# Unread products of the identity in TensorE's pauses, and a new order of all work, in an attention and two-MLP kernel

## The chip, the cores and the metric

The kernel runs on one core of a Trainium2 chip. The metric is the device time of one execution in microseconds. Three runs of the kernel before took 716.44, 717.51 and 718.22 us; the median is 717.51 us.

## The reference, cut to what matters

Three stages follow one another. The first is an attention in both directions between 512 tokens and 32 states, for 4 batches and 8 heads of 64; the other two are MLPs on the 2176 rows that come out of it (4 x 512 tokens and 4 x 32 states, 512 wide).

```python
scores = scale * x @ state.T          # tokens read states, softmax, times state
scores2 = scale * state @ x.T         # states read tokens, softmax, times x
x = concatenate([xread, sread], axis=2)      # 4 x 544 rows of 512
h = x @ w_in                                 # 512 x 2048
x = softplus(h) @ w_out                      # 2048 x 512
g = x @ w_gate; v = x @ w_val                # 512 x 1536 each
out = (silu(g) * v) @ w_out2                 # 1536 x 512
```

The weights are float64 in memory.

## The kernel before, in words

**Arithmetic.** A float32 matrix product is made of three products in a faster format (float32r): each operand is split into a high part (ScalarE copies it into that format) and a low part (VectorE or GpSimd subtracts), and high x high, low x high and high x low are summed. Such a product of 128 x 128 by 128 x 512 is three matmul instructions; a "group" here is six of them (two such products). The weights come as float64, as two 32-bit words each; the steps `size`, `bits` (ScalarE), `head` and `tail` (VectorE) put a float32 together from them before it is split. In the short names of the order these are `ab`, `bt`, `hd`, `tl`, then `wh` (high) and `wl` (low). Some blocks of the MLPs use a scheme with seven products in place of eight, with sums of operands (`g`, `yt`, `at`, `ws`, `sm`).

**The attention.** Items are pairs of a batch (0 to 3) and a parity of heads, numbered 0 to 7: item k is batch k // 2. The steps of an item are, by their short names in the order and their lines: `sc` (L599, TensorE: scores; float32 matmuls, two instructions each, of the two halves of x that `x00` to `x31` load), `mx` and `nm` (L605, L608, VectorE: maximum and its negative), `e` (L612, ScalarE: exponential and its sum), `rc` (L618, L619, VectorE: reciprocals of both items of a batch), `ts` (L625, VectorE: the scores transposed in squares of 32), `M` (L628), `mi` (L632, GpSimd or VectorE: minus the maximum), `ex` (L637, ScalarE), `S` (L640), `r` (L644, L645), `ti` (L649, GpSimd or VectorE), `tu` (L655, transposed back), `ah` (L659, ScalarE: high part), `al` (L662, GpSimd or VectorE: low part); and for the states `pa` (L667, TensorE: four transposes with the identity), `a` (L671, ScalarE), `pr` (L679, TensorE: 16 small products with x in its other layout, `n00` to `n31`), `sr` (L688, ScalarE), `st` (L692, TensorE) and `so` (L698, ScalarE).

**The first MLP.** The attention's last product is folded into the first weights: `mm.cb` (L708, TensorE) multiplies the states of batch b with the c-th 512 columns of w_in, `mh` and `ml` (L712 on ScalarE, L716 on VectorE) split the result. Unit n stands for 512 of these columns c, a batch b and 128 columns of them; `p` n (L756) makes its product (six matmuls, operands from `mh`, `ml`, `ah`, `al`), `sp` n (L738, L743, ScalarE) the softplus, `gl` n (L764, GpSimd) its low part, and `P` n (L780, or L890 in the seven-product scheme) the product with w_out; `ya` to `yd` add the results to the accumulators (L792, L794). `p0` to `p3`, the units of the first batch, are the first split products of the kernel; `P0` follows them. The states take a path of their own (`s1`, L948; `s3`, L968).

**The second MLP.** The `q` products (L1005) take the weights of gate and value from a copy that the kernel has written to DRAM in split form and reads back (`lg`, L518, four loads of 512 KB; `lw`, L522, and `ls`, L568, for the last weights). `a`, `b`, `c` steps and `as`, `bs`, `cb` (L1247, L1264, L1266, L1270) form silu(g) * v, `th` and `tL` (L1011, L1018) split it, `om` (L1042) and `op` (L1066) multiply it with w_out2 and `oA`, `oa` (L1030) add. The path of the states is L1090 to L1130.

**The order.** ORDER is a written-out list of all steps, made ahead of time, and it is the order of every engine's queue and of the DMA queue of SyncE (SP), which starts all loads and stores (L382 and L386 for x, L396 for the weights, `ld.` in the order). Each engine works through its own steps in that order and waits where an operand is not there. A `!` behind a name sends a step to the other of its two engines: steps that are on GpSimd by default (`mi`, `ti`, `al`, `wl`, `sm`, `sl`, `gl`, `gL`, `yl`, `tL`, `wsl`, `cb`, `os.l`, `os.s`) go to VectorE, those on VectorE by default (`ws`, `g`, `yt`, `at`, `os.w`) to GpSimd. HOMES says where each tile lies: eight PSUM banks (`b`), and rooms in SBUF of two sizes (`k`, `d`). Tiles on one line of HOMES share a room one after the other, so a load waits in SP's queue until the tile before it in its room has been read.

Of the kernel before, what the change touches and what calls it, by code (L numbers as in the profile page):

```python
# [17 lines left out]
P = 128  # L18

ORDER = (  # L20
# [174 lines left out]
    ),  # L195
# [1172 lines left out]
```

## Time and profile before

| | |
|---|---|
| median of three runs | 717.51 us (716.44 to 718.22) |
| the profiled execution | 716.6 us, its span 714.8 us |
| TensorE matmuls busy | 699.1 us (98%) |
| VectorE, ScalarE, GpSimd busy | 577.3, 400.3 and 144.6 us |
| moved by DMA | 134.88 MB |

The span is the time from the first to the last instruction on the core; the execution's own time has 1.8 us more around it. PE is TensorE's matmuls, PEld its loading of the stationary operand, DVE is VectorE, ACT ScalarE, POOL GpSimd, SP SyncE's queue. "idle before" is the time that an engine stood before an instruction, with what released it. The granted clock is given as a share of 2.4 GHz, so that 0.50 is 1.2 GHz.

### The profile page before, as it was taken

How to read it: one execution, taken by the hardware profiler on the slowest of the kernel's cores; microseconds unless marked ns; L12 is line 12 of the kernel's file. 1: busy time of each engine (PE TensorE's matmuls, PEld its weight loads, DVE VectorE, ACT ScalarE, POOL GpSimd, SP SyncE). 2: the span in 40 equal slices, each digit the busy share in tenths (PEclk: the TensorE clock that was granted, in tenths of full speed). 3: DMA queues.
4: the chain of work that ended last, by engine and by line, in shares of the span. 5: the costliest groups of instructions: out<-in, count | busy, mean ns of one | idle time of the engine just before them, and what ended most of it. 6: DMA issues, size and time to landing. Idle time of an engine off the chain costs nothing.

```text
span 714.8 us, 10171 instructions
## 1 busy us (share of the span) xinstructions
PE 699.1 (98%) x3618; PEld 555.9 (78%) x3618; DVE 577.3 (81%) x993; ACT 400.3 (56%) x740; POOL 144.6 (20%) x122
## 2 busy tenths in 40 slices
PE   5999999999999999999999999999999999999997
PEld 1478877786878777888888888888888788888886
DVE  4886735899999999889768788868986789967776
ACT  3897664767676767567555654654543344333231
POOL 0244324223562314150101000001020210101101
PEclk9699999999999999999999999999999999999999
DMA  8970000334342500454864757565959889974603
GB/s 336 380 282 19 1 1 28 92 111 156 117 147 91 200 36 1 142 211 149 292 237 157 255 207 277 217 224 209 318 181 351 309 316 357 323 263 160 277 1 118
DMA packets 48626, 134.88 MB, mean 189 GB/s; under 512 B 5440, under 2 KB 17728, under 8 KB 48576
## 3 DMA queue, kind: packets, MB, share of 16 engines
q1 hardware_dynamic: 48576, 134.24, 52.8%
q8 instruction: 28, 0.46, 0.3%
q14 instruction: 22, 0.18, 0.1%
HBM read 93.06 MB, written 41.16 MB: 188 GB/s over the span
## 4 chain that ended last, share of the span: by engine, by line
PE 92%; DVE 3%; DMA 3%; ACT 1%; issue 0%; SPq 0%; ACTq 0%; DVEq 0%
PE b L1005 31%; PE b L890 16%; PE b L756 12%; PE b L1042 11%; PE b L1066 6%; PE b L780 6%; PE b L1090 2%; PE b L948 2%; PE b L708 2%; PE b L968 2%; PE b L1123 1%; DMA k<-gv_d 1%; DMA k<-in_xn_dram 1%; DMA k<-in_xt_dram 1%; PE b L599 1%
## 5 line engine op out<-in xcount | busy, mean ns | idle before, releaser
L1005 PE MATMUL b<-k,k 128*128 128x512 f32 x1008 | 242.6, 391 | 0.6 <-DMA k<-gv_d 0.5
L1005 PEld LDWEIGHTS b<-k,k 128*128 128x128 f32 x1008 | 187.8, 188 | 40.7 <-DMA k<-gv_d 1.0
L890 PE MATMUL b<-d,k 128*128 128x512 f32 x454 | 113.1, 392 | 0.3 <-DVE k L794 0.3
L890 PEld LDWEIGHTS b<-d,k 128*128 128x128 f32 x454 | 84.4, 188 | 24.1 <-issue 3.4
L756 PE MATMUL b<-k,k 128*128 128x512 f32 x384 | 94.8, 393 | 0.0
L1247 DVE TENSOR_TENSOR d<-b,d 128x512 f32<-128x512 f32 x96 | 65.3, 685 | 27.2 <-PE b L1005 16.8
L1264 ACT ACTIVATE d<-b 128x512 f32<-128x512 f32 x72 | 42.4, 593 | 79.2 <-PE b L1005 65.1
L756 PEld LDWEIGHTS b<-k,k 128*128 128x128 f32 x384 | 71.2, 188 | 18.8 <-issue 3.4
L1030 DVE TENSOR_TENSOR k<-b,k 128x512 f32<-128x512 f32 x110 | 73.5, 684 | 14.6 <-PE b L1042 8.4
L1042 PE MATMUL b<-d,k 128*128 128x512 f32 x336 | 82.2, 390 | 0.0
L1042 PEld LDWEIGHTS b<-d,k 128*128 128x128 f32 x336 | 62.8, 188 | 13.0
L1011 ACT ACTIVATE d<-d 128x512 fp32r<-128x512 f32 x63 | 38.4, 625 | 45.7 <-DVE d L1247 34.4
L764 POOL TENSOR_TENSOR d<-d,d 128x512 fp32r<-128x512 f32 x31 | 43.6, 1418 | 93.0 <-ACT d L743 36.8
L419 DVE SCALAR_TENSOR_TENSOR d<-d,k 128x512 int32<-128x512 int32 x66 | 47.3, 727 | 18.3 <-ACT k L413 18.2
L794 DVE TENSOR_TENSOR k<-b,k 128x512 f32<-128x512 f32 x84 | 56.2, 683 | 5.0 <-PE b L890 4.6
L432 ACT ACTIVATE k<-d 128x512 fp32r<-128x512 f32 x51 | 32.0, 629 | 36.9 <-DVE d L426 13.8
L1066 PE MATMUL b<-d,k 128*128 128x512 f32 x210 | 52.0, 390 | 0.0
L1066 PEld LDWEIGHTS b<-d,k 128*128 128x128 f32 x210 | 39.3, 188 | 8.5 <-DVE k L1030 0.4
L1018 DVE TENSOR_TENSOR d<-d,d 128x512 fp32r<-128x512 f32 x55 | 40.5, 739 | 6.6 <-ACT d L1011 6.4
L780 PE MATMUL b<-d,k 128*128 128x512 f32 x192 | 45.1, 390 | 0.0
L413 ACT ACTIVATE k<-k 128x512 int32<-128x512 uint32 x68 | 44.9, 673 | 0.0
L780 PEld LDWEIGHTS b<-d,k 128*128 128x128 f32 x192 | 35.8, 188 | 7.6 <-POOL d L764 0.2
(175 smaller groups left out, 949.1 us busy)
## 6 DMA issues: line engine op xcount, KB each, us to landing
k<-gv_d SPq DMA_DIRECT2D x60, 512.0 KB, 7.9
gv_d<-k SPq DMA_DIRECT2D x48, 512.0 KB, 3.5
k<-in_moe_w_out_dram SPq DMA_DIRECT2D x28, 512.0 KB, 5.3
k<-w_d SPq DMA_DIRECT2D x23, 512.0 KB, 7.6
k<-in_moe_w_in_dram SPq DMA_DIRECT2D x16, 512.0 KB, 6.5
k<-in_moe_w_gate_dram SPq DMA_DIRECT2D x48, 128.0 KB, 3.5
k<-in_moe_w_val_dram SPq DMA_DIRECT2D x48, 128.0 KB, 3.6
w_d<-k SPq DMA_DIRECT2D x12, 512.0 KB, 3.8
```

Of the source, the lines that this page charges most:

```text
L413: nc.scalar.activation(self.bot, low_word, AF.Copy, bias=-0.5 + 7.5 * 2.0 ** -18, scale=2.0 ** -29 * (1 - 2.0 ** -18),)
L419: nc.vector.scalar_tensor_tensor(out=ti, in0=ti, scalar=3, in1=self.bot, op0=ALU.logical_shift_left, op1=ALU.bitwise_or,)
L756: nc.tensor.matmul(ps, halves[s3], others[t3], start=par == 0 and n3 == 0, stop=par == NPAR - 1 and n3 == 2)
L764: eng.tensor_tensor(out=l, in0=sp[u].g, in1=sp[u].h.bitcast(F32), op=ALU.subtract)
L780: nc.tensor.matmul(yps[c, b, dt], halves[s3], t[t3], start=ft == 0 and n3 == 0, stop=ft == FT - 1 and n3 == 2)
L794: nc.vector.tensor_tensor(out=v, in0=ps, in1=v, op=ALU.add)
L890: nc.tensor.matmul(ps, halves[s3], g[t3], start=part in OPENS and f == 0 and n3 == 0, stop=f == 1 and n3 == 2, skip_group_check=True)
L1005: nc.tensor.matmul(ps, halves[s3], others[t3], start=first and i == 0 and n3 == 0, stop=i == 1 and n3 == 2, skip_group_check=True)
L1030: nc.vector.tensor_tensor(out=v, in0=ps, in1=v, op=ALU.add)
L1042: nc.tensor.matmul(ps, halves[s3], act[n + f, j][t3], start=f == 0 and n3 == 0, stop=f == 1 and n3 == 2)
L1066: nc.tensor.matmul(ps, halves[s3], act[n, t][t3], start=opens and n3 == 0, stop=n3 == 2, skip_group_check=True)
L1247: eng.tensor_tensor(out=o(), in0=x(), in1=y(), op=op)
```

## The change

**Unread products.** A step `warm.N.NAME` multiplies the 128 x 128 identity with itself N times (float32) into the bank of the tile NAME, which nothing reads before the tile's own first product overwrites it. There are six in the order: `warm.5.sc0_0` ahead of `sc0`, `warm.8.pa2_1` ahead of `pa5`, `warm.2.pa1_0` ahead of `pa2`, `warm.5.pr2_0` ahead of `pr4`, `warm.1.pm0_0_0` ahead of `mm.00` and `warm.2.pr1_0` ahead of `pr2`; 23 products.

**The order and the homes.** The list has the same 2235 steps beside these six, in another order, and every tile may have another home (41 large rooms and 20 small ones, where there were 40 and 21). 96 steps change between VectorE and GpSimd: 55 go to GpSimd and 41 to VectorE.

**The first addition to an accumulator** is found from the order (the first step that comes) and no longer from the column block c.

The diff, cut to the new function and the part of the order up to the first split products:

```diff
 ORDER = (
-    "x00 st x01 x20 x21 x10 ld.w00 x11 ld.w03 x30 sc0 x31 sc1 ts0 mx0 ld.w02 sc5 nm0 M0 e0 mi0! ld.w01 mx1 ex0 sc4",
-    "mx5 n20 nm1 nm5 S0 e5 pa0 mx4 e1 pa5 nm4 ts5 a0 n21 ab.w00 pa1 ts4 e4 ts1 n11 a5 pa4 rc4 M1 a1 sc3 M5 bt.w00",
-    "mi1 n00 M4 a4 sc2 ab.w03 mx3 mi4 n01 sc6 bt.w03 ts3 ex4 nm3 mx2 ex1 ts2 n10 e3 nm2 S1 e2 pa3 mx6 sc7 n31",
-    "ab.w02 r0 bt.w02 pa2 nm6 mx7 e6 hd.w03 ld.o00 ab.w01 pa6 nm7 ti1! e7 hd.w02 bt.w01 pa7 hd.w00 pr4 a2 hd.w01",
-    "ld.o01 a3 n30 pr5 tu1 sr4 a7 mm.00 rc2 M2 a6 ld.o03 mi2! sr5 mh.000 st2 pr3 M3 so2 mh.001 mm.02 rc0 mi3 ld.o02",
-    "ml.000 ex2 mh.020 S2 ti0 pr0 mh.021 ts7 pr1 ah1 mi5 ts6 mm.01 ex3 ml.001 sr1 al1 sr0 tu0 ex5 pr2 ml.021 sr3",
-    "ah0 st0 pr7 sr2 al0! so0 mh.011 st1 p0 ld.o12 rc6 S3 so1 ld.w11 ab.o00 ml.011 ld.o10 bt.o00 p2 ld.o11 sr7",
-    "hd.o00 ab.o01 ld.w12 r2 wh.o00 p1 S5 ti2 sp0 ml.020 pr6 ti3! p3 wl.o00! ld.w20 ld.e1.0 tu2 sr6 gl0 bt.o01 tu3",
...
+    "x00 st x01 x20 x21 ld.w00 ld.w03 x10 x11 x30 warm.5.sc0_0 sc0 x31 sc1 ts0 mx0 ld.w02 sc4 nm0 mx1 e0 ld.w01 nm1",
+    "M0 pa0 e1 sc5 mx4 a0 n20 rc0 ab.w00 mx5 bt.w00 nm5 nm4 ts4 n21 e5 ts5 e4 warm.8.pa2_1 pa5 M4 n11 pa1 ab.w03",
+    "pa4 ts1 mi4 bt.w03 sc2 M1 a4 sc3 mi0 a5 mx2 a1 n10 mx3 sc6 mi1 ex0 n01 ts2 ex4 nm3 hd.w03 n00 e3 sc7 nm2 mx6",
+    "e2 rc4 n31 ex1 nm6 ts3 warm.2.pa1_0 pa2 pa3 ab.w02 M2 ld.o00 ab.w01 mx7 mi2 e6 S1 bt.w01 ld.o01 warm.5.pr2_0",
+    "pr4 nm7 hd.w00 pa6 bt.w02 S0 e7 pr5 hd.w02 sr4 pa7 r0 n30 a2 hd.w01 ld.w21 a7 ti1! a3 warm.1.pm0_0_0 mm.00 sr5",
+    "tu1 ld.o11 mh.000 M3 a6 pr3 rc6 mh.001 mi3 st2 ld.o12 mm.02 ml.000 so2 ah1 ts7 ti0 ex3 ld.o02 ts6 pr1 mh.021",
+    "al1 M5 pr0 mh.020 ld.o03 tu0 sr1 ex2 warm.2.pr1_0 pr2 rc2 ml.001 ah0 mm.01 ld.o10 sr3 al0! sr0 sr2 ml.021",
+    "ab.o00 st1 st0 pr7 mi5! bt.o00 p2 S2 ab.o01 S3 mh.011 p0 so0 hd.o00 so1 ex5 ml.011 ld.o13 wh.o00 ld.w11 r2 p1",
+    "sp0 ld.w12 ti2! ld.w20 wl.o00! pr6 ld.w10 ti3! p3 ml.020 sr6 gl0 bt.o01 sp1 P0 hd.o01 tu2 wh.o01 ld.w13 gl1",
...
     def y_add(c, b, dt):
-        y_put(b, dt, yps[c, b, dt], c == 0)
-
-    def y_put(b, dt, ps, first):
+        y_put(b, dt, yps[c, b, dt])
+
+    begun = set()
+
+    def y_put(b, dt, ps):
+        first = (b, dt) not in begun
+        begun.add((b, dt))
...
+        def warm(n, name):
+
+            ps = bank(name)
+            for _ in range(n):
+                nc.tensor.matmul(ps[:, :P], ident, ident, start=True, stop=True)
+
+        for names in ORDER:
+            for name in names.split():
+                if name.startswith("warm."):
+                    op(name, warm, int(name.split(".")[1]), name.split(".")[2])
```

The loads `lg13`, `lg15`, `lg16`, `lg21`, `lg1`, `lw0`, `lw12`, `lw13` and `ls0`, of which the prediction speaks, stand in the second half of the order.

## Rows read from the trace of the kernel before

**Rows 1.** The page, part 1: busy time of each engine.

```profile
PE 699.1 (98%) x3618; PEld 555.9 (78%) x3618; DVE 577.3 (81%) x993; ACT 400.3 (56%) x740; POOL 144.6 (20%) x122
```

**Rows 2.** Busy time by stage: stretch, length, engines, granted clock, DMA share, GB/s.

```profile
9.84:39.10 29.26, 24.59 (x355) 11.41 (x352) 25.91 (x57) 23.36 (x53) 6.44 (x6) 0.77 0.89 348
...
140.00:340.00 200.00, 199.42 (x996) 157.00 (x995) 188.69 (x308) 136.57 (x248) 66.41 (x55) 1.00 0.36 123
```

**Rows 3.** TensorE's three waits from 39 us on, first and last: total, times, longest.

```profile
PE b L1005 <- DMA k<-gv_d: 0.5, 1, 0.5
...
PE b L890 <- ACT d L864: 0.3, 1, 0.3
```

**Rows 4.** TensorE by stretch of the attention: length, busy, granted clock, DMA share, GB/s.

```profile
4.83:13.40 8.57, 7.44 (x36) 1.00 0.99 374
...
16.90:30.20 13.30, 11.60 (x89) 0.50 0.99 389
31.00:39.10 8.10, 7.28 (x211) 1.00 0.63 235
```

**Rows 5.** Forms on TensorE in 0 to 13.4, 13.6 to 16.8, 16.9 to 30.2 us: busy, mean ns.

```profile
L599 PE MATMUL b<-k,d 64*32 64x512 f32 x32 | 6.4, 1056 | 6.0 <-DMA d<-in_st_dram 4.8 <-DMA k<-in_xt_dram 1.1
...
L667 PE MATMUL b<-ident,d 128*128 128x128 f32 x8 | 1.3, 287 | 1.5 <-ACT d L612 1.5
...
L599 PE MATMUL b<-k,d 64*32 64x512 f32 x32 | 5.6, 1058 | 0.0
```

**Rows 6.** Timeline of VectorE in the attention: start, length, instruction, idle before.

```profile
9.84 0.72 DVE L625 STREAM_TRANSPOSE d<-b 128x512 f32<-128x512 f32 x1 [9.84 <-PE b L599]
...
12.56 1.28 DVE L605 TENSOR_REDUCE mx<-b 128x1 f32<-128x512 f32 x2
...
20.54 0.69 DVE L605 TENSOR_REDUCE mx<-b 128x1 f32<-128x512 f32 x1 [0.93 <-PE b L599]
...
25.89 0.69 DVE L605 TENSOR_REDUCE mx<-b 128x1 f32<-128x512 f32 x1 [1.06 <-PE b L599]
...
37.78 0.69 DVE L662 TENSOR_TENSOR k<-d,k 128x512 fp32r<-128x512 f32 x1 [0.32 <-ACT k L659]
38.39 0.16 DVE L618 TENSOR_SCALAR sm<-sm 128x2 f32<-128x2 f32 x1
```

**Rows 7.** Timeline of TensorE in the attention and at the first split product.

```profile
18.54 3.67 PE L599 MATMUL b<-k,d 64*32 64x512 f32 x24
...
25.73 1.97 PE L667 MATMUL b<-ident,d 128*128 128x128 f32 x8
...
32.78 1.09 PE L708 MATMUL b<-d,d 64*32 64x512 f32 x16
33.80 1.10 PE L679 MATMUL b<-k,d 128*32 128x64 f32 x64
...
39.10 4.38 PE L756 MATMUL b<-k,k 128*128 128x512 f32 x18
```

**Rows 8.** Timelines of ScalarE and of GpSimd: `ah0`, and `gl0` ahead of P0.

```profile
37.13 0.62 ACT L659 ACTIVATE k<-d 128x512 fp32r<-128x512 f32 x1
...
44.63 1.30 POOL L764 TENSOR_TENSOR d<-d,d 128x512 fp32r<-128x512 f32 x1 [1.54 <-ACT d L743]
```

**Rows 9.** The chain that ended last, 76 to 84 us: 32 float32 matmuls of 128 columns.

```profile
79.74 3.57 PE b L948 x32
```

**Rows 10.** The same chain, 555 to 580 us, and the page's loads: KB, us to landing.

```profile
554.80 6.35 PE b L1005 x28
...
563.88 6.61 DMA k<-gv_d
...
k<-gv_d SPq DMA_DIRECT2D x60, 512.0 KB, 7.9
```

**Rows 11.** Timeline of VectorE: one L419 alone, one while GpSimd works.

```profile
40.79 0.69 DVE L419 SCALAR_TENSOR_TENSOR d<-d,k 128x512 int32<-128x512 int32 x1 [0.86 <-ACT k L413]
...
45.44 1.04 DVE L419 SCALAR_TENSOR_TENSOR d<-d,k 128x512 int32<-128x512 int32 x1
```

More of the change, by code (lines that the diff above doesn't have):

```diff
@@ L893, in y_part_add @@
         j, m = TO[part]
-        y_put(2 * q + j, 2 * m + i, ypx[c, q, part, i], c == 0 and part in ("P1", "P5", "P6", "P4"))
+        y_put(2 * q + j, 2 * m + i, ypx[c, q, part, i])
     ysum = {}
```

520 rows, old and new, of tables (HOMES, ORDER) are left out of this document.

## The prediction

> **What bounds the kernel now.** I read the page's totals first, then the stages, then TensorE's own waits, and last the attention, instruction by instruction. TensorE is busy for 699.1 us of the 714.8 us span [rows 1], so only what shortens its work or its pauses can shorten the run. After the first split product (L756, at 39.10 us [rows 7]) its pauses that carry a releaser come to 1.1 us in three waits [rows 3]. Everything else, some 14 us of pauses and of slow running, lies ahead of 39.10 us. What follows is a fixed list of products, the same in both kernels: whatever makes the first product start earlier moves the whole list, one for one, as long as the list then runs without new pauses.
>
> So the question is what holds the first product back. In the stage up to it VectorE is busy 25.91 us of 29.26, ScalarE 23.36, and TensorE is "busy" 24.59 at a mean granted clock of 0.77 [rows 2]. The clock column says 1.00 up to 13.4 us, 0.50 from 16.9 to 30.2, 1.00 from 31 [rows 4]. The durations correct the first of these: a score matmul takes 1056 ns before 13.4 us and 1058 ns where 0.50 is granted, while the transposes between 13.6 and 16.8 us take 287 ns and four of them up to 1 us in the slow stretch [rows 5, 7]. TensorE therefore worked at 1.2 GHz in both, and at 2.4 GHz only from about 13.6 to 16.9 us and again from 31. The Trainium skill's TensorE: Matmul & The Clock Gate (Part 1, Seeing it yourself) warns not to trust every clock event of a trace; by that, too, the durations decide. The same page calls the cost of the slow start under 1% of a typical span, which as an estimate would be a ceiling of 7.1 us here.
>
> VectorE's queue is what ends last. It begins when scores 0 are out (9.84 us), and its step `al0`, the last operand of the first product, ends at 37.78 + 0.69 = 38.47 [rows 6]. In between stand 38 steps of 0.60 each (two in a row take 1.28 with the last 0.68 long [rows 6]) and some twenty short ones, 25.4 us in all; the other 3.2 are waits. Two of them, 0.93 and 1.06, are waits for scores that TensorE made at the slow clock [rows 6].
>
> **The change, part by part.**
> *Unread products.* Six places, 23 products of 128 columns in float32, two instructions each. The nearest row is L948: 32 such instructions in 3.57 us, so 0.22 us a product at the full clock [rows 9], 0.45 at half: 5.1 to 10.3 us in all. Where TensorE waits anyway they cost nothing: five ahead of `sc0` lie before the first loads land; eight ahead of `pa5` lie where the exponential `e5` is still to come; seven ahead of `pa2` and `pr4` likewise. Three stand in the dense stretch behind `hd.w01` and count in full, 0.7 us. If the cover is gone (slow clock, exponentials already there), each is paid; that is the second rival.
>
> *VectorE's queue up to `al0`.* `mi0` and `mi2` go to GpSimd, `S2` and `ml.021` go behind `al0`: 4 x 0.60 = 2.4 us less. The pair `rc6` comes ahead: 0.3 more (0.16 and a gap [rows 6]). The scores 2, 3, 6, 7 are asked for later by VectorE (`mx2` is the 17th step, `mx6` the 23rd) and, at the full clock, made sooner: eight matmuls take half of 1.09 us against a third of 3.67 [rows 7]. Counting along the queue `mx2` comes at about 19 us with its scores ready near 18.3, so the two waits of 2.0 us go. Scores 0 end in two passes of 1.056 us; at the full clock VectorE would start 1.0 earlier. Bounds 0 and 1.0; in the kernel before the clock was not up by then [rows 5], but five products now come ahead, so I take a little under half, 0.4. Sum: 2.4 - 0.3 + 2.0 + 0.4 = 4.5; `al0` ends at 34.0. The other 1.2 us of waits I leave in the sum; one of that size now stands at `mx5`, for scores 5.
>
> *TensorE's queue behind it.* `hd.w01` stands ten steps and two pairs ahead of the end of `al0`, so it ends near 27.4. From there the new order has three `mm` of 1.09, five `pr` of 0.55, three `st` of 0.3 and three unread products of 0.22 [rows 7, 9], 7.5 us: the first product at 34.9, **4.2 us earlier**. It is the product of unit 2, then 0 and 1; all three need the same operands.
>
> *ScalarE, what is late next.* The first output product P0 needs `gl0`, which ran on GpSimd from 44.63 to 45.93 us [rows 8], with no slack to spare. It follows `sp0` on ScalarE, which follows `ah0` (37.13 [rows 8]). Between `ah0` and `sp0` the new order has `ex5` and one `sr` more: 0.6 and 0.15, by the 0.62 of that row and a quarter of it. So `gl0` ends at 45.93 - 4.5 + 0.75 = 42.2, and the gain that is left is **3.75 us**.
>
> *Loads, SP's queue.* The first loads keep their places but for x10, which goes two back. The weights w02 now wait for the home of x00 and n20, n21 for those of x20, x21, so they are issued a few us later; with the DMA share at 0.99 through 30.2 us [rows 4] the queue behind them is never empty long, and n20 has until `pr4`. o00 comes into the home of x30, free after `sc7`, thus some five us sooner. I cost this at nothing; if n20 were late, `pr4` would hold the four TensorE steps behind it. The two-sided bound is -0.3 to +1.
>
> *All later work.* Of the steps that may run on either engine 55 go from VectorE to GpSimd and 41 back, mostly between 100 and 700 us. VectorE is at 188.69 of 200 us there at its fullest [rows 2] and is relieved by 14 x 0.68, about 9 us over the run; that may take back the two waits of 0.3 [rows 3], or nothing: 0. Loads come nearer to their use. Counted in product groups of six matmuls (28 in 6.35 us [rows 10], so 1.36 a group), three loads stand less than 7 us ahead of their product in the order before (`lg13` 2.7, `lg15` 5.4, `lw13` 5.4), and eight in the new one (`lg15` 2.7, `lw13` 4.1, `lw12`, `lg16`, `lg21` 5.4, `lg1`, `ls0`, `lw0` 6.8). A landing takes 7.9 us, and the one that made TensorE wait took 6.61 [rows 10]. The shortfalls against 7.9 sum to 10.2 us before and 19.8 after; SP runs ahead of the order, so that the 10.2 cost 0.5 [rows 3]. In that ratio the new ones cost 1.0: **0.5 more**. The far ends are 0 and the whole 9.6.
>
> The first-add flag of the accumulators is now found at build time; the same instructions come out: nothing.
>
> Sum: -3.75 + 0.5 = -3.25. The profiled execution took 716.6 us (span 714.8 and 1.8 around it), 0.9 below the median of 717.5: 713.3 on its own time, **714.3 us** on the median.
>
> **The rivals.**
> *Loads or ScalarE take the gain back (chance 0.25, no difference).* If a third of the far end of the loads' shortfall is paid, 3.2 instead of 0.5, the run comes to 717.0. For it: eight close loads where there were three; SP's queue is in order. Against: it ran ahead before. A smaller form of it is GpSimd in VectorE's way. With GpSimd busy from 44.63 to 45.93 the step L419 took 1.04 us instead of 0.69 [rows 8, 11]; `mi0` and `mi2` now run on GpSimd among three `hd` steps, which would cost 3 x 0.35 = 1.05 and give 715.3. The Trainium skill's SBUF — State Buffer (Who interferes with whom) has the two engines share a port pair as an exclusive lock, and a VectorE instruction with two SBUF inputs blocked for it; the row agrees.
>
> *The unread products stand in the way at the slow clock (0.13, slower).* Place: TensorE between `sc5` and `mm.00`. If it stays at 1.2 GHz until 31 us, as it did before, then `sc5` ends at 9.84 + 3 x 1.22 + 1.0 = 14.5 (`sc1`, `sc4`, a transposed tile, `sc5`), and from there come eight products (3.6), three transposed tiles (3 x 1.0, from 8 in 1.97 [rows 7]), four scores (4 x 1.22), two products and two tiles (2.9) and five products (2.2): 31.1 us. At the full clock follow two `pr` and two tiles (2.4) and the 7.5 from above: first product at 41.0, 1.9 later than now, and with the 0.5 for loads 719.9. It decides from about 4 us of slow time more than I assume. Against: TensorE's pauses of the kernel before, during which the clock fell, are just where the products are put.
>
> *The products do nothing for the clock, but are hidden* would leave VectorE's 2.1 us alone, less 0.75 and 0.5: 716.7, also no difference; it is within the 0.25.
>
> **How the numbers follow.** A measurement of this kernel tells about 0.3%, 2.15 us, from no change. The forecast holds 0.62, faster; no difference 0.25; slower 0.13. Within the forecast the start of VectorE (0.6 more), `ex5` (0.75) and the loads (0.5) reach down to 712.4, and some of the 1.2 us of waits left alone to 711.8. Upward the range takes in the no-difference cases and part of the slower one: 718.4. The likeliest case's own range is 711.8 to 715.4.
>
> **What would show it.** Right: score matmuls near 530 to 600 ns for items 2, 3, 6 and 7; VectorE without its two waits on scores; `al0` ending near 34 and the first L756 near 35 us; P0 near 42; TensorE's pauses after that at 1 to 2 us, behind DMA. Wrong: the first L756 after 37 us, the products of the identity running on with `e5` long done, or several us of TensorE waits on loads in the second half.

## The result and the profile after

The change made the kernel **slower**: 726.28 us median of four runs (725.06 to 728.65) against 717.3 us (716.44 to 718.22), a ratio of 1.0129 [1.01, 1.0158]. The profiled execution took 725.95 us with a span of 723.8, which is 9.0 us more than before.

The page's busy line, the stages of [rows 2], and TensorE's waits from 40 us on, to be held against [rows 1 to 3]; all three from the kernel after (its lines are numbered some three lower; the unread products are L1329).

```profile
PE 708.7 (98%) x3664; PEld 563.8 (78%) x3664; DVE 569.7 (79%) x958; ACT 403.5 (56%) x740; POOL 176.0 (24%) x157
```

```profile
9.69:40.57 30.88, 27.63 (x392) 16.54 (x388) 25.76 (x57) 23.57 (x53) 7.49 (x7) 0.94 1.00 390
140.00:340.00 200.00, 199.46 (x1004) 157.22 (x997) 186.80 (x293) 137.78 (x250) 81.77 (x72) 1.00 0.33 113
```

```profile
PE b L1006 <- DMA k<-gv_d: 2.6, 6, 1.3
PE b L1067 <- DMA k<-w_d: 1.3, 1, 1.3
PE b L949 <- ACT d L740: 0.2, 1, 0.2
PE b L1006 <- DVE d L1248: 0.2, 1, 0.2
```

VectorE lost 7.6 us of work and GpSimd got 31.4, as the diff says. The stage up to the first split product did not shrink, it grew from 29.26 to 30.88 us, although the granted clock in it rose from 0.77 to 0.94. (That column is too high at its start: the eight unread products from 15.04 us on took 0.45 us each, which is 1.2 GHz by [rows 9]; only the three transposed tiles from 18.60 on, 1.47 us, ran at 2.4 GHz.) And TensorE now waits on loads in seven places behind it where there was one.

TensorE's timeline in the attention, against [rows 7]:

```profile
12.13 1.11 PE L664 MATMUL b<-ident,d 128*128 128x128 f32 x4
13.18 1.93 PE L596 MATMUL b<-k,d 64*32 64x512 f32 x8
15.04 3.73 PE L1329 MATMUL b<-ident 128*128 128x128 f32 x16
18.60 1.47 PE L664 MATMUL b<-ident,d 128*128 128x128 f32 x12
20.00 1.95 PE L596 MATMUL b<-k,d 64*32 64x512 f32 x32
...
30.96 2.08 PE L705 MATMUL b<-d,d 64*32 64x512 f32 x16
...
40.57 4.37 PE L753 MATMUL b<-k,k 128*128 128x512 f32 x18
```

VectorE's waits in it, `hd.w01` (29.37) and `al0` (37.49), against [rows 6]:

```profile
15.21 0.69 DVE L602 TENSOR_REDUCE mx<-b 128x1 f32<-128x512 f32 x1 [1.78 <-PE b L596]
...
19.24 0.72 DVE L622 STREAM_TRANSPOSE d<-b 128x512 f32<-128x512 f32 x1 [0.96 <-PE b L664]
...
21.14 1.29 DVE L602 TENSOR_REDUCE mx<-b 128x1 f32<-128x512 f32 x2 [0.46 <-PE b L596]
...
29.37 0.63 DVE L416 SCALAR_TENSOR_TENSOR d<-d,k 128x512 int32<-128x512 int32 x1
...
37.49 0.69 DVE L659 TENSOR_TENSOR k<-d,k 128x512 fp32r<-128x512 f32 x1 [0.23 <-ACT k L656]
```

The first product starts at 40.57 instead of 39.10, so 1.5 of the 9.0 us are lost up to it. From it to the end of the span it is 683.2 us where it was 675.7: the other 7.5 lie behind. Matmul by matmul the kernel after is 1.7 us behind where the kernel before stands at 540 us, and 7.5 at the end, so most of it is lost in the last quarter. TensorE's timeline shows the two worst places, against [rows 10]:

```profile
562.82 1.66 PE L1067 MATMUL b<-d,k 128*128 128x512 f32 x6 [1.31 <-DMA k<-w_d]
...
657.47 0.94 PE L1006 MATMUL b<-k,k 128*128 128x512 f32 x3 [0.41 <-DMA k<-gv_d]
659.71 8.48 PE L1006 MATMUL b<-k,k 128*128 128x512 f32 x29 [1.31 <-DMA k<-gv_d]
```

SP's timeline around the second place: first the kernel after, then the kernel before. The four transfers in one row are one `lg`, here `lg21`.

```profile
642.80 0.32 SPq L519 DMA_DIRECT2D k<-w_d  x1
...
650.28 0.32 SPq L519 DMA_DIRECT2D k<-w_d  x1
650.70 2.13 SPq L515 DMA_DIRECT2D k<-gv_d  x4
```

```profile
634.80 4.92 SPq L518 DMA_DIRECT2D k<-gv_d  x4
```

After the change `lg21` stands behind `lw23` (642.80) and `lw22` (650.28), which wait for rooms: SP stood 10.2 us before the one and 3.7 before the other. Its first transfer was issued at 650.70, where before it was issued 15.9 us sooner, and the chain that ended last runs through its landing:

```profile
651.13 8.54 DMA k<-gv_d
```

### The profile page after: what moved, and what is told of

It reads as the page before. It is cut to its first block, busy times and chain, and to the rows that moved or that the text cites. A ratio compares the mean times of both kernels' runs of the same rounds, so it can differ in the third digit from the quotient of the medians.

```text
span 723.8 us, 10283 instructions
## 1 busy us (share of the span) xinstructions
PE 708.7 (98%) x3664; PEld 563.8 (78%) x3664; DVE 569.7 (79%) x958; ACT 403.5 (56%) x740; POOL 176.0 (24%) x157
## 4 chain that ended last, share of the span: by engine, by line
PE 80%; DVE 7%; DMA 5%; SPq 2%; issue 1%; ACT 1%; POOL 0%; ACTq 0%; DVEq 0%
PE b L1006 25%; PE b L891 13%; PE b L753 11%; PE b L1043 9%; PE b L1067 6%; PE b L777 6%; DMA k<-gv_d 3%; PE b L949 2%; PE b L1091 2%; PE b L705 2%; PE b L969 2%; DVE k L795 1%; SPq L393 1%; PE b L1124 1%; DVE d L1248 1%
## 5 line engine op out<-in xcount | busy, mean ns | idle before, releaser
L1006 PE MATMUL b<-k,k 128*128 128x512 f32 x1008 | 245.0, 393 | 3.0 <-DMA k<-gv_d 2.6
L891 PE MATMUL b<-d,k 128*128 128x512 f32 x366 | 97.3, 391 | 0.0
L753 PE MATMUL b<-k,k 128*128 128x512 f32 x384 | 95.0, 393 | 0.0
L891 PEld LDWEIGHTS b<-d,k 128*128 128x128 f32 x366 | 68.2, 188 | 15.6 <-POOL d L872 0.5
L1043 PE MATMUL b<-d,k 128*128 128x512 f32 x308 | 78.2, 391 | 0.0
L1043 PEld LDWEIGHTS b<-d,k 128*128 128x128 f32 x308 | 57.3, 188 | 12.7 <-DVE d L1019 0.7
L1012 ACT ACTIVATE d<-d 128x512 fp32r<-128x512 f32 x58 | 35.8, 628 | 51.0 <-DVE d L1248 22.2
L1067 PE MATMUL b<-d,k 128*128 128x512 f32 x202 | 51.0, 390 | 1.3 <-DMA k<-w_d 1.3
L1067 PEld LDWEIGHTS b<-d,k 128*128 128x128 f32 x202 | 37.8, 188 | 9.7 <-DMA k<-w_d 1.7
L1019 DVE TENSOR_TENSOR d<-d,d 128x512 fp32r<-128x512 f32 x47 | 33.0, 707 | 14.6 <-ACT d L1012 13.9
L1019 POOL TENSOR_TENSOR d<-d,d 128x512 fp32r<-128x512 f32 x10 | 13.4, 1340 | 127.1 <-ACT d L1012 117.1
L891 PE MATMUL b<-k,k 128*128 128x512 f32 x138 | 42.6, 394 | 0.0
```

What stands on the lines that cost most here:

```text
L753: nc.tensor.matmul(ps, halves[s3], others[t3], start=par == 0 and n3 == 0, stop=par == NPAR - 1 and n3 == 2)
L891: nc.tensor.matmul(ps, halves[s3], g[t3], start=part in OPENS and f == 0 and n3 == 0, stop=f == 1 and n3 == 2, skip_group_check=True)
L1006: nc.tensor.matmul(ps, halves[s3], others[t3], start=first and i == 0 and n3 == 0, stop=i == 1 and n3 == 2, skip_group_check=True)
L1019: eng.tensor_tensor(out=l, in0=src(), in1=h.bitcast(F32), op=ALU.subtract)
L1043: nc.tensor.matmul(ps, halves[s3], act[n + f, j][t3], start=f == 0 and n3 == 0, stop=f == 1 and n3 == 2)
L1067: nc.tensor.matmul(ps, halves[s3], act[n, t][t3], start=opens and n3 == 0, stop=n3 == 2, skip_group_check=True)
```

## The experiments

The theories at the start: A, the unread products stand in the way at the slow clock; B, the new order of the attention is late by itself; L, loads of the second MLP come too late because SP's queue holds them. Ratios are to the kernel before on the same chip (716.0 to 716.5 us median); "excess" in the expectations is the time between matmuls beyond their 0.227 us. Each run's kernel has its own line numbers: in the rows below L943, L947 and L949 are the `q` products, L694 the `p` products, L892 the step `s1`, L1004 the `op` products, L343 the step `size`, L538 the scores, L564 and L606 the steps `ts` and `pa`.

**The products.** Taken out of the kernel after (all six), and put into the kernel before at the same steps:

```diff
-x10 x11 x30 warm.5.sc0_0 sc0 ... e4 warm.8.pa2_1 pa5 ... warm.2.pa1_0 pa2
+x10 x11 x30 sc0 ... e4 pa5 ... pa2
```

> The changed kernel without its 23 products of the identity; order and homes as changed. Theory A (the products stand in the way): the eight ahead of item 5's transposes ran from 15.04 to 18.60 us at 1.2 GHz while the exponential they precede was out at 16.9; without them those transposes start near 17.0, the scores of items 2 and 3 near 18.5 instead of 20.0, and the first split product comes 1 to 2 us earlier than 40.57 us: total 724 to 725. Theory B (they keep the clock up, the new order itself is late): without them the granted clock stays at 0.50 for longer than the 3.4 us between 25 and 29 us, the first split product comes at 41 us or later: total 727 to 729.

> The kernel before with the same six groups of products of the identity put ahead of the same steps, order otherwise untouched. Theory A: eight products at half clock delay item 5's transposes, which started at 14.96 us, by 1 to 3 us; the first split product comes at 39.5 to 41 us instead of 39.10: 718 to 719.5. Theory B: the clock does not fall between 17 and 31 us, the scores of items 2, 3, 6 and 7 come 2 us earlier, the first split product at 36 to 38 us: 714.5 to 716.5.

Measured: 725.39 us, 1.0131 [1.0109, 1.0154], without them; 717.47 us, 1.0016 [1.0001, 1.0032], with them in the kernel before. They cost 0 to 1.2 us and are not the loss; theory A falls as its main cause. What they do for the clock is told by the stretch of [rows 4] that stood at 0.50, in the kernel after and then without the products:

```profile
16.90:30.20 13.30, 11.21 (x145) 8.89 (x143) 11.62 (x26) 10.77 (x25) 4.15 (x4) 0.87 1.03 408
```

```profile
16.90:30.20 13.30, 9.24 (x132) 5.71 (x132) 11.73 (x26) 11.59 (x27) 4.12 (x4) 1.00 1.02 407
```

The clock came up without them as well: the other seven profiles of this order without products have 0.87 here, as with them. At the start of the stretch the column is again too high; three transposed tiles there took 1.47 us with the products and 2.82 without, so the clock came up about 1 us sooner with them. In the kernel before with the products the same stretch stands at 0.75; without them five profiles of that order (two with `mi0` and `mi2` moved) have 0.50, 0.50, 0.55, 0.78 and 0.83, so one profile does not tell what the products did there.

**Three loads.** In the kernel after, with and without the products, three moves free loads in SP's queue: the stores `s3d.5` go behind `lw12` and `lw13`, the load `lw22` behind `lg21`, and `os.w21`, a sum on VectorE for whose room `lg15` waits, comes earlier:

```diff
-q7.13 s3d.5 om.10.12 ... lw12 q1.14 lw13 b2.12 ... q5.14 os.w21 lg15 ... ls3 ... lw22 oa.18P10 lg21
+q7.13 om.10.12 ... lw12 q1.14 lw13 s3d.5 b2.12 ... q5.14 lg15 ... ls3 lg21 ... lw22 oa.18P10
```

(`os.w21` then follows `oA.10.13`.)

> The changed kernel with three steps moved: the loads of gate and value weights 21 directly behind the loads ls3 (instead of behind the load of w2_22, which waits for a room), the store step of the states' output s3d.5 behind the loads of w2_12 and w2_13, and the sum os.w21, for whose room the loads of 15 wait, four steps earlier on VectorE. Theory L (the second half's loss is SP's queue holding these loads): TensorE's waits behind gate, value and output weights fall from 3.9 us to under 1, the second stretch at half clock (660.3 to 663.5 us, 1.6 us lost) goes: 4 to 6 us less, 720.5 to 722.5. Rival (the DMA engines are simply full there, share 0.88 to 0.99, whatever is issued first): the wait moves to another load, total within 1 us of 726.3.

> Both edits: no products of the identity, and the three steps for the loads. If A and L hold the two add up: 5 to 8 us below the changed kernel, 718.5 to 721. If B and L hold: 721 to 724.

Measured: 722.82 us, 1.0099 [1.0072, 1.0126], and 721.4 us, 1.0083 [1.0055, 1.0111]. Three moves give back 2.1 us with the products and 3.4 without (by the ratios): L holds for at least a part. With the products TensorE's waits on loads fell only from 3.9 to 2.8 us, where under 1 was expected: those at 657 and 659 are gone, the one near 563 is there still, with 2.0. Between the two runs the products cost 1.1 us, with overlapping intervals.

**Which part of the order.** Two hybrids, both without products: the steps up to P0 in one kernel's order, then all others in the other's. Tiles whose room no longer fits move.

```diff
-ORDER as in one kernel
+ORDER up to P0 as in the other kernel, and then what is left, as in the first
```

> The steps up to P0 in the order of the kernel after (without its unread products), all the others in the order of the kernel before; tiles laid into rooms anew where the mixed order wants it. Theory F (the new order of the attention is worth nothing, and the loss comes from the order behind it): within 1.5 us of the kernel before, 716 to 718. Rival P (the new order of the attention does bring the forecast 3.25 us, and the rest gives them back): 713 to 714. Rival Q (the attention itself is where the time goes): 721 or more.

> The mirror: the steps up to P0 in the order of the kernel before (no unread products), all the others in the order of the kernel after. Theory F: the loss is here, 722 to 725. Rival P: 728 or more, since the gain of the attention is missing too. Rival Q: 716 to 718.

Measured: the new attention in front of the old rest 717.7 us, 1.0021 [1.0011, 1.0031]; the old attention in front of the new rest 729.66 us, 1.0188 [1.0173, 1.0203]. The new attention gains nothing and costs about 1.5 us (in other rooms for 40 tiles); most of the loss is behind it. The second number has a flaw: at the seam TensorE waits 1.49 us on ScalarE at 73.95, which neither kernel does.

The same with the seam at the turn of the states' sums, near 310 us. The first try moved 138 tiles to other rooms, the second let each half keep its own rooms and moved three.

> All steps up to the turn of the states' sums (tys, near 310 us) in the order of the kernel after, without its unread products; the second MLP with its loads and stores in the order of the kernel before. If the late loads of the second MLP carry the loss (theory L): 717 to 719, and TensorE's waits on loads behind 300 us are back at some 0.5 us. If the order of the first MLP carries it: 721 to 725.

> As the run before it of this kind (all steps up to the turn of the states' sums in the order of the kernel after, without unread products; the second MLP in the order of the kernel before), but with each half in the rooms that it has in its own kernel (three tiles moved instead of 138), so that waits on rooms behind VectorE are gone. Theory L: 717.5 to 719.5, TensorE's excess behind 300 us back at some 3 us. If the order of the first MLP carries the loss: 721 or more.

The first try, 737.96 us, 1.0304 [1.0284, 1.0325], tells nothing of the order: TensorE waits on VectorE and GpSimd for rooms between 100 and 340 us. The second came to 719.25 us, 1.0035 [1.0024, 1.0045], and TensorE's waits from 40 us on are down to two, neither above 0.3 us:

```profile
PE b L892 <- ACT d L683: 0.3, 1, 0.3
PE b L949 <- DMA k<-gv_d: 0.3, 1, 0.3
```

So the second MLP's part of the new order carries 0.0096 of the 0.0131, about 6.9 us.

**The loads' order alone.** The kernel after, without products, and every load as many product groups ahead of its first reader as in the kernel before:

> The kernel after without its unread products, and every load of the second MLP set as far ahead of its first reader (in TensorE work) as it stands in the kernel before, as far as its stores allow (14 tiles change rooms for it). Theory L (the late loads carry the loss behind the attention): TensorE waits on loads behind 300 us for under 1 us in all, the time falls from some 725 to 719 or 720, and what is left above the kernel before lies ahead of 150 us. If the loss is in the order of the engines' work instead: 723 or more.

> As the run with the leads of the kernel before in the kernel after (no unread products), but only tiles that loads fill change rooms (11 of them); the tiles of VectorE's and ScalarE's results keep the rooms of the kernel after. In the earlier run TensorE no longer waited on loads behind 360 us, while two waits on ScalarE, at 72 and 350 us, took more than that gave. Theory L (the order of the loads carries the loss behind the attention, and those two waits came from the rooms): both waits are gone, the time is 719 to 720.5. If the two waits belong to the earlier loads themselves: 726 or more again.

Measured: 727.79 us, 1.0159 [1.0131, 1.0187], and 726.27 us, 1.013 [1.0111, 1.015]. Both took away every wait on a load behind 360 us, and both met a new one; TensorE's timeline of the second:

```profile
355.12 2.93 PE L947 MATMUL b<-k,k 128*128 128x512 f32 x6 [5.98 <-ACT d L1206]
```

I had put such a wait in the first of the two runs down to the rooms; they were not its cause. The chain of the same kernel leads from ScalarE to a load of w_out2, which now stood in SP's queue behind `lg2` and `lw0`:

```profile
341.19 10.72 DMA k<-in_moe_w_out_dram
...
352.00 0.09 ACT d L343
```

So these first four loads stay, and only the later ones move (the loads in SP's order):

```diff
-lg12 lg13 lg14 lw12 lw13 ls0 lg15 ls1 lg16 lw14 lw15 lw17 lw16 lg17 lg18 ls2 lw18 lg19 lw19 lg20 lw23 ls3 lw22 lg21 lw21 lg22 lg23 ls4 lw20
+lg12 lg13 ls0 lg14 lw12 lw13 ls1 lg15 lw14 lg16 lw17 lw15 lg18 lg17 lw16 lg19 lw18 ls2 lw19 lg20 lw20 ls3 lg21 lw21 lw22 lg22 lg23 ls4 lw23
```

> As the run before it, but the four loads that start the second MLP (lg0, lg1, lg2, lw0) stay where the kernel after has them: in that run they stood in SP's queue ahead of a load of w_out2 whose conversion ScalarE needed at 352 us, and TensorE waited 6 us there. The other loads keep the leads of the kernel before. Theory L: the wait at 349 us is gone, TensorE waits on loads behind 360 us for under 0.5 us, and the time is 718.5 to 720, level with the run that has the whole second MLP of the kernel before (719.25). Otherwise 723 or more.

Measured: **719.48 us, 1.0051 [1.0035, 1.0068]**: 5.7 us less than without the move, by the order of the loads and new rooms for 11 tiles that loads fill, with every other step in place, and level with the run that had the whole second MLP of before. TensorE waits 0.2 us on loads in all, so the rival that the DMA engines are simply full, whichever load goes first, falls. Where TensorE stood still at 657 and 659 us it now runs 48 matmuls on end; SP issued that load at 642.93 (two rows, TensorE's and SP's timelines):

```profile
651.70 11.04 PE L947 MATMUL b<-k,k 128*128 128x512 f32 x48
```

```profile
642.93 1.74 SPq L456 DMA_DIRECT2D k<-gv_d  x4
```

The mirror gives eleven loads of the kernel before the short leads of the kernel after, but leaves most of SP's order as it was:

```diff
-lg21 q1.20 ... q4.20 at.18T2 lw22
+q1.20 ... lg21 ... q4.20 at.18T2 lw22
```

> The mirror, with nothing else changed: the kernel before with eleven loads of the second MLP set as close to their first readers as they stand in the kernel after (lg15 from 5.4 to 2.7 us of TensorE work, lg21 from 10.9 to 5.4, lw12 from 12.3 to 5.4, lw0 from 22 to 6). Theory L: 719.5 to 722, with waits of 1 us and more on loads near 560 and 660 us. If late loads are hidden here, as the prediction had it for most of them (0.5 us): 717 or less.

Measured: 717.64 us, 1.0014 [0.9998, 1.0029]. Far below the 719.5 to 722 that L had for it: the short leads alone cost 1 us by the medians (0 to 2 by the interval), and TensorE waits 0.8 us on loads in all. `lw23` and `lw22` still stand behind `lg21` there, and SP issued it 6.8 us sooner than the kernel after did:

```profile
643.90 2.23 SPq L519 DMA_DIRECT2D k<-gv_d  x4
```

**The attention.** Two steps of the kernel before move to GpSimd, and nothing else; and in the hybrid with the new attention three scores move ahead:

```diff
-nm0 M0 e0 mi0! ... ld.o03 mi2!
+nm0 M0 e0 mi0 ... ld.o03 mi2
```

```diff
-M0 pa0 e1 sc5 ... e4 pa5 ... sc2 M1 a4 sc3
+M0 sc5 pa0 e1 ... e4 sc2 sc3 pa5 ... M1 a4
```

> The kernel before with two steps of the attention, mi0 and mi2, on GpSimd in place of VectorE, and nothing else. By the step of the prediction that took 0.6 us of VectorE's queue for each: al0 ends 1.2 us earlier and the kernel is some 1 us faster, 715 to 716 against 716 to 717. By the rival (VectorE only waits longer for the scores and for TensorE behind them): no change of the time, al0 ends within 0.3 us of before, and the wait of 0.93 us ahead of the maximum at 20.54 us grows by about 0.6.

> The attention in the order of the kernel after (no unread products) and the rest in the order of the kernel before, as in the run of the front alone (717.7), with three score steps moved ahead on TensorE: sc5 ahead of pa0, sc2 and sc3 ahead of pa5. If VectorE's waits of 1.81 and 2.14 us for these scores are what ate the forecast gain: both waits shrink to under 1 us, the first split product starts 1 to 3 us earlier than 39.24, and the time is 715 to 716.5. If it is the loads of x that make the scores late: the waits stay, 717 to 718.5.

Measured: 715.94 us, 0.9993 [0.9984, 1.0003], and 718.2 us, 1.0023 [1.0009, 1.0038]. With the two steps on GpSimd `hd.w01` ends at 28.19 instead of 29.65, and the first split product starts 1.06 us earlier; the time gains 0.5, inside the interval. The profile does not tell the two steps from the clock: the granted clock stood at 0.50 for 6.8 us there and for 13.7 in the kernel before's, and the wait of 1.06 for scores is gone where these took 1.06 us in place of 1.93. `al0` ends at 38.01, only 0.46 earlier and not 1.2, since VectorE now waits 1.16 for ScalarE's `mh.000`. With the scores ahead VectorE's two waits for them go, and others come: TensorE waits 2.09 for x and VectorE 2.60 for TensorE (the two timelines of that kernel, one row each):

```profile
13.92 3.13 PE L538 MATMUL b<-k,d 64*32 64x512 f32 x16 [2.09 <-DMA k<-in_xt_dram]
```

```profile
18.13 0.72 DVE L564 STREAM_TRANSPOSE d<-b 128x512 f32<-128x512 f32 x1 [2.60 <-PE b L606]
```

`al0` ends at 36.53 there, 1.9 earlier than in the kernel before, and the first product at 38.85 only 0.25 earlier: TensorE's own list behind `hd.w01` sets it, not `al0` (1.15 us of that list are a pause that the profile puts to issue).

**A version faster than both.** The kernel before with the two steps on GpSimd and two loads earlier:

```diff
-e0 mi0! ... mi2! ... q1.12 ... lg13 ... op.12P1 ... lg15
+e0 mi0 ... mi2 ... lg13 q1.12 ... lg15 op.12P1 ...
```

> A version that might beat both: the kernel before with mi0 and mi2 on GpSimd, and lg13 and lg15 two TensorE steps earlier, so that lg15 stands ahead of the stores that held it in SP's queue until 563.4 us (one tile changes its room). The wait of 0.9 us near 570 us goes and the first split product starts some 1 us earlier: 714.5 to 715.5 against 716.5. If the end of the attention is set by TensorE's list and not by VectorE: 716.

Measured: **715.1 us, 0.9978 [0.9966, 0.999]**, 1.3 us less than the kernel before by the medians. Its first split product starts at 36.70. The order up to there is that of the run with the two steps alone, which had 38.04, so 1.3 us of it are the difference between two executions. Near 570 us, where [rows 10] have a landing of 6.61 us on the chain and TensorE waited 0.5 for it [rows 3], its timeline has no gap:

```profile
36.70 4.35 PE L694 MATMUL b<-k,k 128*128 128x512 f32 x18
...
564.04 4.24 PE L943 MATMUL b<-k,k 128*128 128x512 f32 x18
568.12 1.52 PE L1004 MATMUL b<-d,k 128*128 128x512 f32 x6
569.48 5.60 PE L943 MATMUL b<-k,k 128*128 128x512 f32 x24
```

**The sum.** By ratio, from the kernel after down: products 0 (1.0129 to 1.0131; up to 1.2 us in the other two pairs); late loads 0.0080, **5.7 us**; the rest of the second MLP's order 0.0016; the first MLP's 0.0014; the attention's 0.0021. The loads' share is 3.7 to 7.7 us by the two intervals that it comes from. The last three are 1 to 1.5 us each, with intervals about as wide as they are; their sum, 3.7 us (2.5 to 4.9), is surer. The parts are parts of the order with the rooms that go with it.

## Why the prediction was wrong

*Where the miss lies.* The forecast was -3.25 us and the profile has +9.0. Two steps failed, by about the same amount: the loads (0.5 us forecast, 5.7 measured) and the attention (a gain of 3.75 forecast, a loss of 1.5 measured). The rest of the order, put at nothing, cost some 2.2 us, and why is not shown.

*What bounds the kernel: right, but used too simply.* TensorE sets the time. "A fixed list of products, the same in both kernels" held for the work and not for its pauses, and these, with the slow clock behind one of them, made five sixths of the loss.

*Loads of the second half: the first step that failed.* I counted each load's distance to its product, put the shortfalls at 0.5 us "in that ratio" because "SP runs ahead of the order", and gave 9.6 as the far end. It was 5.7. The mirror fits this count where SP's order stays mostly as it was: short leads cost 0 to 2 us there. In the new order `lw23` and `lw22` wait for rooms ahead of `lg21`, four stores of the states' output stand ahead of `lw12` and `lw13`, `os.w21`, for which SP stood 4.6 us in the midst of `lg15`; SP cannot run ahead of what it waits for. I looked at the lead and not at who stands in front. The Trainium skill's DMA: Bandwidth & Descriptors (Issuing engines are not separate DMA queues) says that issuing from several engines saves only the sequencer's issue time, usually small beside the transfer. The trace agrees for the issue itself, 0.32 us for `lw23`, and no run here issues loads from a second engine; the 10.2 us that SP stood before `lw23` are a wait, which that sentence does not count.

*VectorE's queue, the second step that failed: 4.5 us forecast at `al0`, 0.3 measured.* It ended at 38.18 and not at 34.0. The 2.4 us of work left the queue, but the step "the two waits of 2.0 us go" failed. `mx5` waits 1.78 for scores 5, which the new order has TensorE make behind `pa0` (12.13 us) and which take 1.93 at the slow clock; scores 2, 3, 6 and 7 come at 20.00 and not near 18.3, behind eight products and three transposed tiles; and `ts1` waits 0.96 for its room. In all VectorE waits 4.6 us where I left 1.2. So `hd.w01` ended at 30.00: forecast 27.4, before 29.65. I had counted each queue, but not TensorE's order against what VectorE asks of it. GpSimd was not in VectorE's way: the four `hd` steps took 0.63 to 0.68 us, none while GpSimd worked.

*TensorE's list behind `hd.w01`: 7.5 us forecast, 10.6 measured.* `mm.00` took 2.08 for 1.09, its second half held by a bank that ScalarE had to read first; an unread product waited 0.54 for its own bank, and 0.63 went in issue (0.36 before), and some 0.7 of earlier steps was still to do when `hd.w01` ended. The gain of 4.2 us became a loss of 1.5.

*ScalarE and P0.* With the first product late P0 came at 46.95, not at 42.2; `gl0`, of which I said that it would be late next, ended at 47.0, and TensorE did not wait for it. In the run with the scores ahead it waited 0.97 us for the next one, `gl1`.

*The unread products: 0.7 us forecast, 0 to 1.2 measured.* The size is about right, but in part by luck: the 0.7 were three others, and the eight that should have been hidden ran on when their cover was gone. They took from 15.04 to 18.6 at half clock, 0.45 us each, while `e5` was out at 16.9:

```profile
16.18 0.69 ACT L609 ACTIVATE d<-b,nm 128x512 f32<-128x512 f32 x1 [1.18 <-DVE nm L605]
```

So far the rival had it, and its first product at 41.0 was closest to the 40.57 measured; but it had the slow clock last until 31 us, and the clock came up at about 18.6, so its number is luck too. Most of the 5.7 us between the 34.9 of the forecast and 40.57 is not the products': without them the first product came between 38.7 and 40.4 in the eight profiles that have the new order up to P0.

*Early loads: costed at nothing*, and nothing is seen of them in the kernel after, where TensorE waits 0.98 us for x at 7.7 us (1.13 before). But they were a bound that I did not see: with the scores moved ahead TensorE stood waiting for x.

*VectorE's relief between 100 and 700 us: nothing forecast*, and no gain was seen: the order there cost some 2.2 us beside the loads.

## What to carry to other kernels

Where one queue issues all loads in order, a load's lead is counted from the moment that everything ahead of it in that queue can be issued: a load that waits for its room, or a store that waits for its data, makes every load behind it late. A planned order is read against each pair of engines that hand work to each other; steps taken off one queue only turn into waits if what the next step needs is no earlier. When an order is rewritten, the far end is read as closely as the part it was rewritten for: here most of the loss lay near 560 and 660 us.

## What the runs showed of the hardware

**A short pause can cost twice.** Behind the waits of 0.41 and 1.31 us near 659 the granted clock fell to 1.2 GHz for a while. By the stages of the kernel after it was 0.57 between 660 and 664 us, with 12 matmuls in 4.00 us, where [rows 10] have 28 in 6.35 at the full clock, thus 2.72 for 12: another 1.3 us. Behind the single wait of 1.31 near 563 it stayed at 1.00 (first of the rows here):

```profile
562.00:568.00 6.00, 5.18 (x23) 4.30 (x24) 4.77 (x9) 0.78 (x2) 1.67 (x1) 1.00 0.90 281
```

```profile
653.00:660.00 7.00, 5.28 (x22) 3.78 (x22) 2.63 (x5) 1.20 (x2) 1.26 (x1) 1.00 1.00 327
660.00:664.00 4.00, 4.00 (x12) 3.09 (x12) 1.19 (x2) 1.12 (x2) 0.00 (x0) 0.57 1.03 416
```

The Trainium skill's TensorE: Matmul & The Clock Gate (Loop structure matters more than you think) has a long wait for DMA between every two matmuls as what makes the engine run cold. The trace agrees in kind, but here two short waits came before the fall. In the same kernel without the products it fell behind a wait of 2.01 us near 562 and not behind one of 1.22 near 659; what decides is not shown.

**Rooms weigh as much as order.** The same order of steps took 737.96 us with 138 tiles moved to other rooms and 719.25 with three moved: 18.7 us for the choice of which buffer holds what (the second has one large room more).
